# Chunk-selecting attention and a softplus feed-forward on one core: entries of a written-out order moved, four given to another engine, filler matmuls counted anew

## The chip, the cores and the metric

One core of one Trainium2 chip runs the whole program. The metric is the device time of one execution in microseconds (us); of several executions the median is taken. The engines are named as the profile names them: PE (TensorE, matmuls; PEld its weight loads), DVE (VectorE), ACT (ScalarE), POOL (GpSimd), SP (SyncE, which issues DMAs).

## The reference

Attention over 4 batches, 8 heads, 768 positions and a head size of 64, in which each query sees only the 6 best of its causal chunks of 32 keys, then a feed-forward layer on all 3072 tokens:

```python
k_min, k_max = k_chunks.min(axis=3), k_chunks.max(axis=3)
ub = np.sum(np.maximum(q * k_min, q * k_max), axis=-1)
ub = np.where(causal, ub, -1e9)
top_chunks = np.argsort(ub, axis=-1)[..., -6:]
scores = np.where(sel & (pos[:, None] >= pos[None, :]), scale * q @ k.T, -1e9)
attn = softmax(scores) @ v
x = attn.transpose(0, 2, 1, 3).reshape(B * S, H * D)
h = x @ w_in
out = (np.maximum(h, 0) + np.log1p(np.exp(-np.abs(h)))) @ w_out
```

## The kernel before, in words

The queries are cut into 12 blocks of 256 (block n is batch n // 3, rows n % 3). For each block the operations are: loads (`ld k`, `ld q`, `ld v`), transposes of k and q (`kT`, `qT` on PE for blocks 0 to 2, `kD`, `qD` as DMA transposes from block 3 on), the chunks' maxima and negated minima (`kx`, `kn`, line 508 or 500, on DVE), their copy into the block-diagonal tile `bd` (line 520 on DVE, line 294 on POOL), copies of k (`kc`) and q (`qc`), the positive and negative parts of q (`qpn`, lines 562 to 566), the bounds of the chunks (`ub`, lines 585 and 589, PE), their six largest (`mx`, line 612), the mask (`raw`, lines 627 and 630, tile mraw), its transpose (`mT`, lines 643 and 649, PE) and copies into the rows below q (`mc`). Then come the scores (`s`, lines 703 and 704, PE, 256 and 128 or 256 columns), the exponential (`ex`, line 711, ACT), the causal cut (`af`, line 721, POOL), attention times v (`av`, line 733, PE), the normalisation (`nm`, lines 746 and 747, DVE), the transpose (`oT`, line 764) and the copy to x (`xc`, DVE or ACT). The feed-forward follows block by block: `h` (line 902, 8 matmuls of 256 columns), `e` (line 907) and `ln` (line 912) on ACT, `y` (lines 932 and 847), `ye` (copy out of PSUM) and `st` (store).

Block 0 is made in two halves (pairs of heads 0, 1 and 2, 3), so its operations stand twice as often. Its k and q come through SP as fp32 into the tile wx (`ld k0.0` to `ld q0.1`) and are cast (`cast k0.1` and so on) to the tile io. All other loads are issued by POOL at line 364. `oh` (line 305) makes the rows that SP spreads with `ohk` (line 332) below q and k; block 0's scores wait for them.

The order of the work is written out. The string `ORDER` is a list of words: the first letter names the engine (P, A, V, G for POOL, S for SP), then comes the operation and, with #, which of its kind. Each engine executes its words in the order of the list; waits come from the data alone. A word `z` with a number stands for filler on PE: matmuls of the tile zero into a bank that nobody reads, n // 4 of 512 columns (line 1018) and n % 4 of 128 columns (line 1020). One unit is thus 128 columns. All the z words stand in the first 28 us.

```python
    for o in order:
        if isinstance(o, int):
            wide = T.zero.unsqueeze(1).to_broadcast([128, 4, 128])
            for _ in range(o // 4):
                nc.tensor.matmul(T.pools["y"].homes[0], T.zero, wide, start=True, stop=True)
            for _ in range(o % 4):
                nc.tensor.matmul(T.pools["y"].homes[0][:, 0:128], T.zero, T.zero, start=True, stop=True)
            continue
        o.inst = o.fn(o.eng)
```

Of the kernel before, what the change touches and what calls it, by code (L numbers as in the profile page):

```python
# [206 lines left out]
Gld_q2.1 Gld_v1.0 Ps0#4 Aex0#4 Gld_v1.1 Gaf0 z8 Ps0#5 Aex0#5 Vmx1 Vraw1 z1 Ps0 Gaf0 Aex0 Pav0 Pav0 Gaf0 Gw_in0 Vnm0
Gaf0 PqT2 Gw_in1 Gld_q3.0 Vcm0 Ps0#7 z8 PmT1 Vmc1 Akc1 Ps0 PoT0 Aex0 Aex0 Axc0 Pav0 Pav0 z7 Ps1#12 Aex1#12 PkT2 PkT2
Ps1#4 Vmc1 Gaf0#6 Gaf0 Gaf0 Aex1#4 Vnm0 Gaf0 Gld_k3.0 Gw_in2 PqT2 Ps1#5 Aex1#5 z3 PoT0 Ps1#7 z1 Ps1 Gcm Pav0#6 Pav0#7
Gvone Vkx2 Vkn2 Vnm0#3 Vbd2 Vxc0 Aqc2 Aex1#7 Aex1 z14 Ps1 Aex1 z4 Ps1#3 Vqpn2 Vqpn2 z2 Ps1 Pav0 Pav0 Aex1#3 Gaf1#1  # L210
PoT0#3 Ps1#15 Vnm0 Vkc2 Aex1 Gaf1 z2 Ps1#8 Pub2 Axc0#3 Aex1#15 Ps1#11 Aex1#8 Aex1#11 Gw_in3 PoT0 Ps1#13 Pav1 z2 Ps1#9
# [843 lines left out]
```

## Time and profile before

| what | value |
|---|---|
| median of 3 runs | 252.55 us (252.5 to 253.54) |
| the profiled execution | 251.79 us, of which its span is 250.1 us |
| around the span | 1.69 us |
| PE busy | 244.2 us, 98% of the span |
| ACT, DVE, POOL busy | 210.8, 175.9 and 121.2 us |
| granted TensorE clock, mean | 1.000 |

The page of the profile gives the busy time of each engine and, in 40 slices, its share; PEclk is the granted TensorE clock in tenths of full speed. Busy time of PE counts filler like any other matmul. The timeline lists instructions in order of time, merged where equal ones follow each other: start, duration, engine, line, operation, tiles, and in brackets the idle time just before with what ended it.

### The profile page before, as it was taken

How to read it: one execution, taken by the hardware profiler on the slowest of the kernel's cores; microseconds unless marked ns; L12 is line 12 of the kernel's file. 1: busy time of each engine (PE TensorE's matmuls, PEld its weight loads, DVE VectorE, ACT ScalarE, POOL GpSimd, SP SyncE). 2: the span in 40 equal slices, each digit the busy share in tenths (PEclk: the TensorE clock that was granted, in tenths of full speed). 3: DMA queues.
4: the chain of work that ended last, by engine and by line, in shares of the span. 5: the costliest groups of instructions: out<-in, count | busy, mean ns of one | idle time of the engine just before them, and what ended most of it. 6: DMA issues, size and time to landing. Idle time of an engine off the chain costs nothing.

```text
span 250.1 us, 7021 instructions
## 1 busy us (share of the span) xinstructions
PE 244.2 (98%) x2754; PEld 201.0 (80%) x2770; DVE 175.9 (70%) x570; ACT 210.8 (84%) x387; POOL 121.2 (48%) x197
## 2 busy tenths in 40 slices
...
PEclk9999999999999999999999999999999999999999
...
GB/s 171 153 158 172 192 176 152 196 155 204 114 141 169 179 160 145 148 175 175 152 175 160 86 144 105 64 7 42 12 97 43 35 177 3 1 86 3 0 85 168
DMA packets 113953, 29.88 MB, mean 119 GB/s; under 512 B 103776, under 2 KB 110944, under 8 KB 113920
## 3 DMA queue, kind: packets, MB, share of 16 engines
...
q8 instruction: 21, 0.34, 0.5%
...
## 4 chain that ended last, share of the span: by engine, by line
PE 91%; DVE 4%; ACT 2%; issue 1%; ACTq 0%
PE ph L902 34%; PE py L932 11%; PE pt L847 9%; PE py L847 8%; PE ps L703 6%; PE po L733 6%; PE ps L704 4%; PE pt L703 2%; PE ph L932 2%; PE pt L733 2%; PE py L1018 2%; PE pt L704 2%; PE pt L585 2%; ACT qt L293 1%; DVE kx L508 1%
## 5 line engine op out<-in xcount | busy, mean ns | idle before, releaser
L902 PE MATMUL ph<-x,w_in_sb 128*128 128x256 bf16 x768 | 97.5, 272 | 0.0
L721 POOL TENSOR_SCALAR_AFFINE_SELECT pt<-pt 128x256 bf16<-128x256 bf16 x96 | 41.0, 451 | 85.8 <-ACT pt L711 85.4
L711 ACT ACTIVATE pt<-ps 128x512 bf16<-128x512 f32 (+1 forms) x145 | 75.5, 550 | 7.7 <-PE ps L704 6.8
L902 PEld LDWEIGHTS <-w_in_sb 128*128 128x128 bf16 x768 | 72.4, 98 | 9.0
L907 ACT ACTIVATE e<-ph 128x512 f32<-128x512 f32 x96 | 56.9, 607 | 13.8 <-PE ph L902 13.6
L912 ACT ACTIVATE g<-e 128x1024 bf16<-128x1024 f32 x48 | 50.6, 1066 | 0.4
L932 PE MATMUL py<-w_out_sb,g 128*128 128x512 bf16 (+1 forms) x129 | 31.5, 365 | 0.8
L733 PEld LDWEIGHTS <-pt 128*128 128x128 bf16 x672 | 28.1, 97 | 2.3
L711 ACT ACTIVATE pt<-pt 128x512 bf16<-128x512 f32 (+1 forms) x47 | 26.3, 572 | 4.0 <-PE pt L704 3.3
L500 DVE TENSOR_REDUCE kx<-kT 128x32 bf16<-128x1024 bf16 x18 | 21.5, 1210 | 6.7 <-DMA kT<-io 6.6
L932 PEld LDWEIGHTS <-g 128*128 128x128 bf16 x176 | 16.3, 97 | 11.8
L733 PE MATMUL po<-v,pt 128*128 128x65 bf16 x502 | 23.5, 193 | 0.0
L847 PEld LDWEIGHTS <-g 128*128 128x128 bf16 x224 | 21.2, 98 | 2.6
L364 POOL DMA_DIRECT2D v<-in_v_dram x24 | 22.1, 923 | 0.1
L364 POOL DMA_DIRECT2D io<-in_k_dram x22 | 20.1, 919 | 0.0
L364 POOL DMA_DIRECT2D io<-in_q_dram x22 | 20.0, 913 | 0.0
L703 PE MATMUL ps<-qt,kb 128*128 128x256 bf16 x73 | 19.2, 272 | 0.0
L703 PE MATMUL ps<-qa,ka 96*128 96x256 bf16 x72 | 18.9, 273 | 0.1
L847 PEld LDWEIGHTS <-df 128*128 128x128 bf16 x168 | 16.0, 98 | 1.8
L704 PE MATMUL ps<-qt,kb 128*128 128x256 bf16 (+1 forms) x73 | 17.4, 245 | 0.0
L704 PE MATMUL ps<-qa,ka 96*128 96x128 bf16 (+1 forms) x72 | 16.8, 240 | 0.0
L747 DVE TENSOR_TENSOR osw<-po,rew 128x256 bf16<-128x256 f32 x37 | 15.7, 425 | 1.3
...
## 6 DMA issues: line engine op xcount, KB each, us to landing
...
```

The lines of the kernel that those rows point to most:

```text
L364: lambda e, t=t: nc.gpsimd.dma_start(out=into(nm, n, t), in_=rows(nm, n, t)),
L500: nc.vector.tensor_reduce(kx.ap[:, :, j].rearrange("d p (t c) -> d t p c", t=NT), kT.ap.rearrange("d p x -> d (p x)").rearrange("d (t p c ...
L703: nc.tensor.matmul(sp.ap[:, 0:QB], kk[0:nr, p, j * 128:(j + 1) * 128], qq, start=True, stop=True)
L704: nc.tensor.matmul(sp.ap[:, QB:w], kk[0:nr, p, (j + 1) * 128:(j + 2) * 128], qq[:, 1] if last else qq, start=True, stop=True)
L711: lambda e, sp=sp, pt=pt, h=h, j=j, w=w: nc.scalar.activation(pt.ap[:, h, j:j + 2].rearrange("k j c -> k (j c)")[:, 0:w], sp.ap[:, 0:w], A ...
L721: nc.gpsimd.affine_select(out=d, in_=d, compare_op=ALU.is_ge, fill=0.0, base=0, channel_multiplier=-1, pattern=[[0, 2], [1, 128]])
L733: nc.tensor.matmul(o[:, u, h], pt.ap[:, h, j, c0:c0 + 128], T.V[i][:, j, 2 * p + h, :], start=(j == 0), stop=(j == t0 + u))
L847: nc.tensor.matmul(bank.ap[:, c * HD:(c + 1) * HD], a(f), w(f), start=start and f == 0, stop=f == HF - 1, skip_group_check=True)
L902: nc.tensor.matmul(o[:, j], T.w_in[:, dt, ft * 128:(ft + 1) * 128], x.ap[:, dt], start=(dt == 0), stop=(dt == KDM - 1))
L907: lambda e, hb=hb, eb=eb, f2=f2: nc.scalar.activation(eb.ap[:, f2 * 512:(f2 + 1) * 512], hb.ap, ACT.Exp),
L912: lambda e, eb=eb, g=g, f4=f4: nc.scalar.activation(g.ap[:, f4 * 4:(f4 + 1) * 4].rearrange("f j c -> f (j c)"), eb.ap, ACT.Ln, bias=1.0),
L932: nc.tensor.matmul(yb.ap[:, 0:c1 - c0], g.ap[:, f, u * 128:(u + 1) * 128], T.w_out[:, f, c0:c1], start=(f == 0), stop=(f == KFF - 1))
```

## The change

The list `ORDER` alone changes. The whole diff is two versions of that string; its first lines are

```diff
-Vzero Sld_k0.0 Acast_k0.0 Vmr0#1 Vkb0 Vmr0 Gvone Gident z32 PkT0 PkT0 Sld_q0.0 Vr4 Gc4 Vbd0 Vkx0 Vkn0 Sld_k0.1
-Vcast_k0.1 Acast_q0.0 z2 PqT0 PqT0 Aqc0 Vbd0#2 Gld_k1.0 Gld_k1.1 Vqpn0 Aqpn0 Sld_q0.1 Acast_q0.1 z33 PqT0 PqT0
...
+Vzero Sld_k0.0 Acast_k0.0 Vmr0#1 Vkb0 Vmr0 Gvone Gident z32 PkT0 PkT0 Sld_q0.0 Vr4 Gc4 Vbd0 Vkx0 Vkn0 Sld_q0.1
+Sld_k0.1 Acast_q0.0 z2 PqT0 Voh PqT0 Aqc0 Gld_k1.0 Gld_k1.1 Vcast_k0.1 Vqpn0 Acast_q0.1 z23 PqT0 PqT0 Gld_q1.0
...
```

Four operations go to another engine: the first `qpn0` of the negative part from ACT to DVE, the second half's `bd0` from POOL to DVE, the second `xc0` from DVE to ACT, and the second `ye1` from DVE to ACT. On SP `ld q0.1` now stands before `ld k0.1`, `oh` on DVE before `cast k0.1`, and POOL's `ld q2.0` behind both halves of `ld k2`. Between 45 and 80 us some twenty words move by a few places: `av2`, `s2`, `h1`, `s3`, `h2`, `y1`, `kc3`, `qac3`, `kc4`, `bd3`, `bd5`, `ln2`, `e2`, `ld k6`, `ld q6`, `ld q7.0`, `st1`. The z words before are 32 2 33 21 3 12 31 8 1 8 7 3 1 14 4 2 2 2 (186 units), now 32 2 23 16 4 13 7 1 4 1 9 1 18 4 2 5 2 (144 units).

The first place is DVE from the first chunk maxima of block 0 (tile kx_103 from the PE tile ph_87) to those of its second half (ph_88); io is the cast input, ohb the rows of `oh`, qpos and qneg the parts of q. Before:

```order
L508 TENSOR_REDUCE kx_103<-ph_87 128x2x8 x2
L294 CAST io_95<-wx 128x4x2x64
L520 TENSOR_REDUCE bd_76<-kx_103 64x4x8 x2
L566 TENSOR_SCALAR qpos_109<-qt_106 128x512
L305 SCALAR_TENSOR_TENSOR ohb<-ident 32x768
L508 TENSOR_REDUCE kx_103<-ph_88 128x2x8 x2
```

and with the change, up to the chunk maxima of block 1 (kx_104):

```order
L508 TENSOR_REDUCE kx_103<-ph_87 128x2x8 x2
L305 SCALAR_TENSOR_TENSOR ohb<-ident 32x768
L294 CAST io_95<-wx 128x4x2x64
L566 TENSOR_SCALAR qpos_109<-qt_106 128x512
L564 TENSOR_SCALAR qneg_110<-qt_106 128x512
L520 TENSOR_REDUCE bd_76<-kx_103 64x4x8 x2
L508 TENSOR_REDUCE kx_103<-ph_88 128x2x8
L608 TENSOR_REDUCE ub_111<-pt_91 128x4
L612 MAX ub_111<-pt_91 128x8 x4
L508 TENSOR_REDUCE kx_103<-ph_88 128x2x8
...
L520 TENSOR_REDUCE bd_76<-kx_103 64x4x8 x2
L508 TENSOR_REDUCE kx_104<-pt_92 128x4x8 x2
```

The rows of `oh` move ahead of the cast, the first qneg comes from ACT, and the second half's copy into bd from POOL.

The second place is ACT among the exponentials of block 1 (tile pt from the PSUM tiles ps), with the copy x that DVE had before; one piece of the difference:

```order
 L711 ACTIVATE pt_113<-ps_85 128x512
 L711 ACTIVATE pt_113<-ps_86 128x384
+L293 COPY x_121<-pt_91 128x256
 L293 COPY qt_106<-ph_88 128x1024
 L711 ACTIVATE pt_113<-ps_85 128x384
```

The copy of the transposed output to x stands on ACT now, ahead of the copy of block 2's q.

The third place is POOL's queue at the start, where io are the tiles of loaded k and q, v that of v, and qa the rows of q of block 0; one piece of the difference:

```order
 L364 DMA io_97<-in_k_dram 128x8x64 x2
 L364 DMA io_98<-in_q_dram 128x8x64 x2
-L364 DMA io_99<-in_q_dram 128x8x64
 L294 COPY qa_105<-qt_106 64x512
 L364 DMA v_70<-in_v_dram 128x8x64 x2
 L294 COPY qa_105<-qt_106 64x512
-L294 COPY bd_76<-kx_103 64x4x8 x2
```

The first copy of qa comes one DMA issue earlier, and the copy into bd is gone from POOL.

## Rows read from the trace of the kernel before

**Rows 1.** The page, its slices of the granted clock.

```profile
PEclk9999999999999999999999999999999999999999
```

**Rows 2.** Stretches, all engines: length, busy us (x count) PE, PEld, DVE, ACT, POOL.

```profile
10.00:15.00 5.00, 4.94 (x51) 2.86 (x50) 4.94 (x20) 4.84 (x8) 4.94 (x8) 1.00 1.85 174
15.00:20.00 5.00, 4.95 (x76) 3.52 (x75) 4.75 (x27) 4.39 (x10) 4.61 (x9) 1.00 1.99 130
...
140.00:160.00 20.00, 20.00 (x232) 18.05 (x230) 18.84 (x73) 16.88 (x33) 3.82 (x9) 1.00 0.67 114
```

**Rows 3.** The same stretches, line 1018 alone (filler of 512 columns): PE, PEld busy.

```profile
10.00:15.00 5.00, 3.03 (x13) 0.94 (x11) 1.00 1.85 174
15.00:20.00 5.00, 1.57 (x5) 0.40 (x5) 1.00 1.99 130
```

**Rows 4.** Waits of PE's weight loads: total us, times, longest.

```profile
PEld L585 <- DVE qneg L564: 0.5, 1, 0.5
PEld L643 <- DVE mraw L630: 0.4, 1, 0.4
```

**Rows 5.** Timeline of DVE, from the cast of block 0's k to its second mask.

```profile
6.35 0.42 DVE L294 CAST io<-wx 128x512 bf16<-128x512 f32 x1
6.68 0.36 DVE L520 TENSOR_REDUCE bd<-kx 64x32 bf16<-64x32 bf16 x2
7.08 0.30 DVE L566 TENSOR_SCALAR qpos<-qt 128x512 bf16<-128x512 bf16 x1
7.30 0.94 DVE L305 SCALAR_TENSOR_TENSOR ohb<-ident 32x768 bf16<-32x768 bf16 x1
8.59 1.29 DVE L508 TENSOR_REDUCE kx<-ph 128x16 bf16<-128x512 bf16 x2 [0.35 <-PE ph L481]
...
14.15 0.43 DVE L566 TENSOR_SCALAR qpos<-qt 128x1024 bf16<-128x1024 bf16 x1
...
14.59 0.18 DVE L630 TENSOR_TENSOR mraw<-pt,ub 128x8 bf16<-128x8 f32 x1
```

**Rows 6.** Timeline of DVE, block 2's parts of q.

```profile
24.32 0.29 DVE L294 COPY x<-pt 128x256 bf16<-128x256 bf16 x1
24.65 0.57 DVE L566 TENSOR_SCALAR qpos<-qt 128x1024 bf16<-128x1024 bf16 x1
25.14 0.62 DVE L564 TENSOR_SCALAR qneg<-qt 128x1024 bf16<-128x1024 bf16 x1
```

**Rows 7.** Timeline of ACT, a copy to x and block 4's positive part of q.

```profile
24.99 0.37 ACT L293 COPY x<-pt 128x256 bf16<-128x256 bf16 x1
...
63.60 1.06 ACT L562 ACTIVATE qpos<-qt 128x1024 bf16<-128x1024 bf16 x1
```

**Rows 8.** Timeline of POOL, start and the cuts beside block 2's q.

```profile
5.30 2.82 POOL L364 DMA_DIRECT2D io<-in_q_dram  x3
8.10 0.63 POOL L294 COPY qa<-qt 64x512 bf16<-64x512 bf16 x1
...
24.53 0.95 POOL L721 TENSOR_SCALAR_AFFINE_SELECT pt<-pt 128x256 bf16<-128x256 bf16 x2 [0.76 <-ACT pt L711]
```

**Rows 9.** Timeline of PE: filler, block 2's bounds, scores of block 3, block 4's bounds.

```profile
1.06 3.59 PE L1018 MATMUL py<-zero 128*128 128x512 bf16 x8 [1.06 <-DVE zero L303]
...
5.63 1.89 PE L1018 MATMUL py<-zero 128*128 128x512 bf16 x8
...
25.36 0.19 PE L585 MATMUL ph<-bd,qpos 128*128 128x48 bf16 x1
25.82 0.20 PE L585 MATMUL ph<-bd,qneg 128*128 128x48 bf16 x1 [0.27 <-DVE qneg L564]
...
63.53 0.27 PE L703 MATMUL ps<-qa,ka 96*128 96x256 bf16 x1
...
63.70 0.27 PE L703 MATMUL ps<-qa,ka 96*128 96x256 bf16 x1
...
64.74 0.18 PE L585 MATMUL pt<-bd,qpos 128*128 128x32 bf16 x1
```

More of the change, by code (lines that the diff above doesn't have):

```diff
@@ L207 @@
[L207 to L211, printed above, removed]
@@ new lines @@
+Gld_q1.1 Vqpn0 Vbd0#2 PkT1 Akc0 PkT0 Sohk Sohk PkT0 Vkx0 Aqc0 Aqpn0#3 Pub0 Aqpn0 Sohk#3 Vmx0 Vkn0 Vraw0 Gqac0 Vbd0#3
+Gld_v0.0 Akc0 Gld_v0.1 PkT1 Akc0#3 Vkx1 Gqac0 Sohk z16 PmT0 Amc0#1 PqT1 z4 PqT1 Amc0 Aqc1 Vkn1 Ps0#2 Vcm0 Aex0#2 Pub0
+Ps0 Vbd1 Vkc1 Vmx0 Vraw0 z13 PmT0 Vqpn1 Vqac1 Aqpn1 z7 Pub1 Aex0 Akc0 Gld_k2.0 Gld_k2.1 Vmc0 Ps0 Vmc0 Aex0 Gld_q2.0
+Gld_q2.1 Gld_v1.0 z1 Ps0#4 Aex0#4 Gld_v1.1 Gaf0 z4 Ps0#5 Aex0#5 Vmx1 Vraw1 z1 Ps0 Gaf0 Aex0 Pav0 Pav0 Gw_in0 Vnm0 Gaf0
+Gaf0 PqT2 Gw_in1 Gld_q3.0 Ps0#7 PmT1 Vmc1 Akc1 Ps0 PoT0 Aex0 Aex0 Axc0 Pav0 Pav0 z9 Ps1#12 Aex1#12 PkT2 PkT2 Ps1#4
@@ new lines @@
+Vmc1 Gaf0#6 Gaf0 Gaf0 Aex1#4 Vnm0 Gaf0 Gld_k3.0 Gw_in2 PqT2 Ps1#5 Aex1#5 PoT0 Ps1#7 z1 Ps1 Gcm Pav0#6 Pav0#7 Gvone
+Vkx2 Vkn2 Vnm0#3 Vbd2 Axc0 Aqc2 Aex1#7 Aex1 z18 Ps1 Aex1 z4 Ps1#3 Vqpn2 Vqpn2 z2 Ps1 Pav0 Pav0 Aex1#3 Gaf1#1 PoT0#3
+Ps1#15 Vnm0 Vkc2 Aex1 Gaf1 z5 Ps1#8 Pub2 Axc0#3 Aex1#15 Ps1#11 Aex1#8 Aex1#11 Gw_in3 PoT0 Ps1#13 Pav1 z2 Ps1#9 Pav1
+Gld_k3.1 Aex1#13 Gw_out0 Gaf1#6 Gaf1 Ps1#14 Axc0 Vmx2 Gaf1#7 Vraw2 Aex1#9 Aex1#14 Ph0 Ps1#10 Aex1#10 Ps1 Vnm1 Gaf1
+Vqac2 Aex1 Ae0 Gaf1 Gld_q3.1 PmT2 Vmc2 Ph0 Gaf1 Pav1#6 Pav1#7 Vnm1#3 Vkc2 Ps2#6 Ae0 Gld_v2.0 Aex2#6 Ps2#8 Aex2#8 Ph0#3
@@ new lines @@
+Aln0 Ps2#2 Pav1 Pav1 Ps2 Aex2 Ph0 SkD3 Vnm1 Vmc2 Ps2#12 Pav1 Pav1 Aex2#2 PoT1 Vxc1 Ae0 Vnm1 Ps2#5 Vbd0 Ph0 Aex2#12
+Aex2#5 Ae0 Ps2#17 PoT1#2 Ps2#14 Aex2#17 PoT1 Vxc1 Vxc1 Ph0 PoT1 Vxc1 Ps2 Aex2#14 Ae0 Ps2#9 Ae0 Aex2 Ph0 Ps2#11 Aex2#9
+Gaf2 Aex2#11 Ae0 Gw_out1 Ph0 Ae0 Ps2 Ps2 Gaf2#4 Gaf2 Gaf2 Ph1 Gaf2#5 Ph1#2 Gld_v2.1 Vkx3 Aex2 Aex2 Ps2#18 Aln0 Ps2
+Gwh0 Gw_out2 Vkn3 Pav2 Gw_out3 Aex2#18 Py0 Aex2 Ae1 Ps2 Aln0 Aex2 Ps2#22 Ph1 Ae1 Aex2#22 Gld_k4.0 Gld_k4.1 Gld_k5.0
+Gwh2 Ae1 Gld_q4.0 Py0 Ps2 Gaf2 SqD3 Ph1#5 Pav2 Gld_q4.1 Aln1 Ps2#20 Ph1#4 Aex2#20 Vnm2 Gld_k5.1 Pav2 Ae1#4 Vbd3 Aex2
@@ new lines @@
+PoT2 Ae1#5 Axc2 Pav2 Aln0 Ps2 Aex2 Vqpn3 Ph1 Vqpn3 Vkc3 Pub3 Vuba3 Vnm2 Vmx3 Ph1 Ps2 Aex2 Ae1 Aln1 Vraw3 Py0 Pav2 Pav2
+Ps2#21 Vwv0 Vkc3 Ae1 Ps2#23 Aex2#23 Py0 Gaf2#7 Aye0 Ph1 Ps2 Vqac3 Vwv6 SmD3 Gwh4#1 Gwh2 Gaf2 Aex2#21 Ae1 Aln1 Aex2
+SkD4 Sohk Gwd2 Vnm2 Vwv2 Py0 Py0 Py0 Py0 PoT2 PoT2 Aye0 Vxc2 Axc2 Aln1 Pav2 Pav2 SqD4 Py1 Py1 Py1 Sohk Skb0 Gld_v3.0
+Vnm2 PoT2 Gld_q5.0 Amc3 Ps3#2 Aex3#2 Ps3#6 Aex3#6 Vkx4 Gld_q5.1 Vkn4 Vxc2 Vwh6#1 Py1 Aqpn4 Ps3 Ph2 Vqpn4 Vbd4 Pub4
+Vmc3 Gld_v3.1 Vuba4 Aye1 Ps3#4 Vmx4 Vraw4 Vqac4 Ae2 Ph2 Aex3#4 Aex3 Vkc4#1 Ps3 Gld_q7.0 Vkc4 Py1 Gld_k6.0 Gld_k6.1
@@ new lines @@
+Gaf3#2 Ae2 Aex3 Ps3#7 SkD5 Aex3#7 SmD4 Ph2 Ae2 Gaf3#1 Vkx5 Aln2 Ps3 Sst1 Ph2#4 Ps3 SqD5 Aex3 Ae2#4 Ph2#5 Ae2#5 Vkn5
+Aex3 Gaf3 Gaf3#4 Aln2#2 Pav3 Pav3 Vnm3 Gaf3#7 Gaf3#6 Gaf3#5 Gld_q6.0 Py1 Gld_v4.0 Gaf3 Gld_v4.1 Ph2 Vmc4 Pav3#6 Pav3#7
+Py1 Vnm3#3 Ae2 Ps4 Ps4#8 Ps4#4 Aln2 Ps4#9 Pav3#4 Pav3#5 Ph2 Vbd5 SkD6 Aex4#4 Vmc4 Aex4 Aex4#8 Aex4#9 Vnm3#2 Ps4 Aex4
+Vqpn5 Vqpn5 Pav3 Pav3 Vnm3 Ps4#3 Py1 Pub5 Aex4#3 Aye1 Ps4 Ps4#11 Aex4#11 Gaf4#5 Ph2 Ps4#15 Ps4 Py2 Vuba5 Vmx5 Vraw5
+Gld_v5.0 Py2 Aex4 Ps4#12 Gaf4#1 Gaf4 Ae2 Ae2 Aln2 Vkx6 Aex4 Aex4#12 Aex4#15 Pav4 Ps4#7 Aex4#7 Py2 Ps4#14 Aex4#14 SxD3
@@ new lines @@
+Ps4 Ps4 Ps4 Vqac5 Pav4 Gld_q6.1 Vkc5#1 Aex4#10 Aex4#13 Ph3 Gaf4#4 Vkn6 Gld_k7.0 Aex4 Ph3 Ae3 Ae3 Aln3 Pav4#4 Vkc5
+Ph3#6 Pav4#5 Gld_k7.1 SmD5 Vmc5 Vnm4 Ps5#18 Gld_k9.0 Gaf4#6 Gld_v8.0 Gld_v5.1 SqD6 Gaf4#7 Gaf4 Sst0#1 SkD7 Ps5
+Gld_k9.1 Gaf4 Ps5#19 Aex5#18 Aex5#19 Aex5 Py2 Vmc5 Ps5#23 Pav4#6 Ps5 Vnm4#2 Pav4#7 Vnm4#3 Ps5#4 Ps5 Ae3#6 Ph3#4 Aex5
+Aex5#23 Aex5 Aex5#4 Pav4 Ps5#12 Ps5#20 Pav4 Aex5#12 Aex5#20 Ps5#6 Ps5#14 Aex5#6 Aex5#14 Ph3 Ps5#10 Ps5#21 Gld_q7.1
+Gld_v7.0 Gaf5#7 Gaf5#6 Ps5#8 Ps5#22 Vwh0 Gld_k8.0 Vye2 Vqpn6 Vqpn6 Py2 Vkc6#1 Vwd6 Vnm4 Vbd6 Vwv4 Ae3#4 Aex5#21 Aex5#8
@@ new lines @@
+Aex5#10 Ps5#9 Ph3#5 Ps5#11 Ae3 Pub6 Ph3#7 SxD4 Gaf5#2 Aex5#22 Gld_q9.0 Aex5#11 Ae3#5 Pav5#6 Ph3 Gaf5#3 Gaf5#4 Gaf5
+Ae3#7 Aex5#9 Vwh6 Vqac6 Vuba6 Vmx6 Vraw6 Aln3#3 Vkx7 Ae3 Vkc6 SmD6 Vkn7 Vkc7#1 Vbd7 Vkc7 Vmc6 Ps5#17 Ps5#16 Ps5#15
+Ps5#7 Aex5#7 Aex5#17 Py2 Py2 Aex5#16 Pav5#7 Aex5#15 Aln3 Gld_k8.1 Ps5#13 Ps5#5 Gld_v6.0 Gld_v6.1 Ps5 Aex5#13 Gaf5#5
+Ph4#2 Ph4 Aex5#5 Vmc6 Pav5#4 Aln3 Ae4 Aex5 Py2 Ps6#2 Ps6 Aex6 Gaf5 Gld_q11.0 SqD7 Aye2 Ae4#2 Gld_k10.0 Pav5#5 Gaf6
+Gld_q9.1 Gld_k10.1 Ph4 Pav5 Pav5 Py3 Ps6 Vnm5 Aex6 Aex6 Ae4 Ph4#4 Ps6#6 Ps6#7 Vnm5#2 Vqpn7 Vqpn7 Aex6#6 Ae4#4 Vnm5#3
@@ new lines @@
+Aex6#7 Pav5 Pav5 Ps6 Aex6 Vnm5 Pub7 SkD9 SkD8 Gaf6 Vuba7 Pav6 Ph4 Ps6#5 Pav6 Ps6 Vmx7 Vraw7 Sst2#1 Gaf6#7 SxD5 Gaf6#3
+Ae4 Aex6 Aex6 Py3 Ph4 Gaf6#6 Gaf6 Pav6 Py3 Vkx9 Ph4 Pav6#6 SmD7 Vnm6 Sst2 Sst1 Aln4 Ae4 Gaf6#5 Gaf6 Aln4 Py3 Pav6#7
+Vdl4 Ph4 Pav6#4 Pav6#5 Aln4 Gwd0 Gld_k11.0 Gld_k11.1 Gld_v11.0 Gld_v7.1 Gld_q8.0 Aye3 Pav6 Vqac7 Vnm6#3 Vmc7 SqD9 Vkn9
+Vkc9 Vnm6#2 Py3 Py3 Ps7#4 Ae4 Ae4 Aln4 Vdd4 Vbd9 Vmc7 Vqpn9 Ps7 Aex7#4 Ps7#12 Aex7#12 Ph5 Ps7 Aex7 Ps7#5 Ph5#4 Py3
+Aex7#5 Aex7 Ae5#4 Ae5 Ps7#9 Ps7#8 Aex7#8 Aex7#9 Ph5#2 Ps7 Aex7 Gld_q8.1 Ph5 Ae5 Ps7 Vde4 Vnm6 Aex7 Ps7#11 Gld_q11.1
@@ new lines @@
+Gld_v10.0 Gaf7#1 Ps7#15 Aex7#15 Aex7#11 Ae5 Py3 Aye3 Aln5 Vqpn9 Vkx8 Vkc9 Pub9 Ph5 Vuba9 Vmx9 Ph5 Py4 Py4 Ps7#10 Vwh4
+Gld_v9.0 Gld_v9.1 Gaf7#2 Gaf7 Pav7 Ps7 Vraw9 Vkn8 Pav7 Vwd4 Ae5#5 Ae5 Aex7#10 Py4#4 Py4 Ph5#7 Aex7 Aln5#2 Ps7 Aex7 Ps7
+Ps7 Py4#5 Py4#6 Gaf7#7 Gaf7#4 Gaf7 Aln5 Gaf7 Py4 Vnm7 Vdh4 Py4 Vbd8 Vkc8 Gld_v10.1 Vdf4 Vqac9 Ph5 Pav7 Aex7#14 Ayr4
+Aex7 SxD6 Sst0 SmD9 Vyz4 Vyv4 Vmc9#1 Amc9 Ae5 SkD10 Pav7#4 Pav7 Vnm7 Py4#12 Py4#13 Aye4 SqD8 Pav7 Ps9#2 Py4 Vnm7 Py4
+Ps9#5 Ps9#4 Aex9#2 Aex9#4 Ae5 Aln5 Aex9#5 Ps9#6 Py4 Ph6 Py4 Ayd4 Ae6 Aex9#6 Gld_q10.0 Gld_v8.1 Gaf7 Vkc8 Vdl5 Vyw4
@@ new lines @@
+Vqpn8 Vyc4 Vqpn8 Pav7 Pav7 Ph6#2 Ps9#3 Aex9#3 Ps9#7 Ae6#2 Aex9#7 Pub8 Ph6 Gaf9#4 Py5 Ps9 Ph6#4 Ps9 Py5 Vkx10 Vnm7 Aex9
+Ae6 Vde5 Gld_v11.1 Gld_q10.1 Gyx4 Vyf4 Vdd5 Vuba8 Vmx8 Vraw8 Gaf9#2 Aex9 Ph6#5 Gaf9#3 Py5#4 Py5#5 Gaf9 Gaf9 Pav9
+Sst3#1 SxD7 Gaf9#7 Gaf9 SqD10 SmD8 SkD11 Sst4#1 Sst4 Sst3 Ae6#4 Aln6 Ae6#5 Ph6#6 Ae6#6 Ph6#7 Ae6#7 Pav9#4 Pav9#5 Pav9
+Ayr5 Vdh5 Vkn10 Vkc10 Vbd10 Vnm9 Vnm9#2 Ph6 Vdf5 Ae6 Aln6 Aln6#3 Vqac8 Aln6 Gaf9 Py5#6 Py5#7 Py5#8 Ph7 Pav9 Pav9 Ae7
+Ph7#2 Vyz5 Py5 Vmc8 Vqpn10 Vqac10 Vqpn10 Vmc8 Ae7#2 Ps8#12 Py5 Py5 Ps8#14 Aex8#12 Py5#12 Ps8 Vnm9 Aex8 Ph7 Ps8#9 Vyv5
@@ new lines @@
+Vyc5 Ps8#6 Pav9 Py5#13 Pav9 Aex8#14 Ps8#11 Ae7 Aex8#6 Aex8#9 Py5 Py5 Ps8#18 Aex8#11 Ps8#7 Aex8#7 Vdl6 Vde6 Vye5 Vnm9
+Aex8#18 Ps8#17 Aex8#17 Pub10 Ph7 Ayd5 Ae7 Ps8 Ps8#23 Aex8#23 Aex8 Ph7 Ps8 Aex8 Vdh6 Vyw5 Vuba10 Vmx10 Vraw10 Vyx5 Vyf5
+Vdf6 Gaf8 Gaf8#5 Ph7#6 Ps8#5 Aex8#5 Vdd6 Gaf8 Ae7#6 Ps8#22 Py6 Py6 Py6 Ps8#15 Ps8#16 Ph7#7 Py6#4 Aln7 Aex8#16 Aex8#22
+Ps8#10 Py6#5 Ps8#8 Py6#6 SxD9 Ae7 Aex8#10 Gaf8#3 Gaf8#4 Py6 Ps8#4 Ae7#7 Vkx11 Vkn11 SmD10 Ayr6 Vyz6 Vmc10 Ph9#2
+Aex8#15 Aex8#4 Aln7 Py6 Aex8#8 Vkc11 Vyv6 Vmc10 Gaf8#7 Ph7 Gaf8 Ps8#19 Ps8#21 Aex8#21 Ps8#20 Py6 Py6 Aex8#20 Aex8#19
@@ new lines @@
+Py6#12 Ps8#13 Aex8#13 Ps8 SqD11 Aex8 Gaf8 Ae7 Py6#13 Ps10#12 Py6 Pav8#2 Ayd6 Ae9#2 Vye6 Pav8#3 Pav8 Pav8 Py6 Ps10#13
+Aex10#12 Aln7#3 Aex10#13 Vyw6 Aln7 Vkc10 Vyc6 Ph9#5 Pav8#6 Ps10 Ps10#8 Pav8#7 Vbd11 Vnm8 Aex10 Vnm8 Vyx6 Vyf6 Vnm8#3
+Vdl7 Ps10#3 Ph9#4 Aex10#3 Ps10 Py7 Aex10 Ps10#5 Ps10#4 Ae9#4 Vqpn11 Vde7 Vqpn11 Pav8 Pav8 Ps10#7 Aex10#4 Py7 Aex10#5
+Aex10#7 Vnm8 Vdh7 Vdd7 Vdf7 Pub11 Py7#4 Py7#5 Ps10#11 Aex10#8 Ps10#9 Ph9 Ae9#5 Aex10#9 Aex10#11 Vyr7 Ps10 Ae9 Aex10
+Py7 Ph9 Vuba11 Py7 Ps10 Gaf10#2 Ps10#15 Vmx11 Ae9 Aln9 Gaf10#1 Gaf10#4 Gaf10#6 Gaf10#5 Gaf10#3 Gaf10 SxD8 Sst6#1
```

90 lines of the change are left out of this document (17 added, 73 removed).

## The prediction

> **What bounds the kernel now.** I read the page first, for the clock: the granted TensorE clock stands at its upper level (2.4 GHz) in every slice [rows 1]. Then the stretches: from 140 to 160 us PE is busy all 20.00 us with real work [rows 2], so there the end is set by PE, and a change of order wins only what PE loses before. The longest waits of its weight loads are 0.5 and 0.4 us, on DVE in both [rows 4]. There PE looks just as full (4.94 of 5.00 us from 10 to 15 us), but 3.03 us of that is wide filler [rows 2, 3]. The reader is to see that the filler covers waiting: what PE waits for at 14.6 us is the mask of block 0's second half, DVE's chain [rows 4]. The timeline of DVE shows that chain: one wait of 0.35 us before 8.59 us, then no other until the mask is written at 14.59 + 0.18 us [rows 5]. Up to there the kernel is bound by DVE, then by DVE, ACT and PE in turn, and once the filler ends by PE alone.
>
> **The change part by part.**
>
> *The start of DVE.* Before, DVE goes cast, copy into bd, qpos, rows of `oh`, and then waits for the second half's chunk maxima until 8.59 us [rows 5]. Now `oh` comes first, and qneg (ACT's until now) is added. From one start to the next the rows cost: cast 6.68 - 6.35 = 0.33, bd 7.08 - 6.68 = 0.40, qpos 7.30 - 7.08 = 0.22; `oh` 0.94 alone, about 0.86 where its tail is covered as qpos's is [rows 5]. A 512-wide qneg on DVE is not in the trace; the nearest row is qpos of the same size, 0.22, and I take that. DVE starts at 6.35 and needs 0.86 + 0.33 + 0.22 + 0.22 + 0.40 = 2.03 us, so the second half's maxima start at 8.38 instead of 8.59: **0.21 us earlier**. With the bare 0.94 it is 0.13, and no more than the 0.35 of the idle row can be won. From there to the mask, DVE loses block 1's qpos (14.15, behind the mask now) of 0.34 to 0.43 and gains POOL's copy into bd, 0.36 to 0.40 by the DVE row of that copy, and a small memset: nothing in sum. That qpos is then in front of block 1's bounds, which need it anyway. I put 0.2 us to PE here, with ends 0 and 0.35.
>
> *Filler.* 42 units fewer, 37 of them ahead of this mask or just behind. A unit costs 1.89 / 8 / 4 = 0.06 us [rows 9], so about 2.5 us of matmuls go. I cost them at **nothing**: PE waits for DVE with or without them, and what hid under filler becomes visible waiting. The five words from 18 on in the list (18 4 2 5 2) have 7 units more than before, 0.4 us; they stand where PE waits for ACT.
>
> *The copy to x, DVE to ACT.* Between 24.32 and 25.14 us DVE does this copy (0.29 us, 0.33 from start to start) ahead of block 2's parts of q, and PE waits for the second of them: 25.82 - 25.36 = 0.46 us between two matmuls of 48 columns [rows 6, 9], the 0.5 of the waits [rows 4]. Without the copy that wait shrinks by 0.33, and with the 0.2 from the start all of the 0.46 could go. Against that ACT, which feeds the score banks that PE waits for between 20 and 25 us, takes over a copy of 0.37 [rows 7] there. In sum between -0.46 and 0; I take **-0.25**, as ACT was relieved of the first qneg before.
>
> *Block 4's bounds.* One pair of score matmuls of block 3 moves from in front of the feed-forward group to behind block 4's bounds, so the bounds come 63.70 - 63.53 = 0.17 us earlier on PE: 64.57 instead of 64.74 [rows 9]. They wait for ACT's qpos, which ends at 63.60 + 1.06 = 64.66 [rows 7]. So PE stands still for about **+0.13 us** (0 to 0.17) where it had not; behind it the same matmuls follow, and nothing gives it back.
>
> *The rest.* `ld q2.0` behind `ld k2` frees one POOL issue, 2.82 / 3 = 0.94 us [rows 8], for v and k2: hidden, since PE waits for masks and exponentials there, not for loads. SP's order of the four first loads only exchanges which half is cast first. The moves between 45 and 80 us, and the second `ye1` on ACT, lie under a PE that has no wait to give back: nothing, and if their cover is gone the loss is a wait like that of block 4.
>
> **The sum.** -0.2 - 0.25 + 0.13 = -0.32 us, from -0.81 to +0.17. The profiled execution took 251.79 us (its span of 250.1 and 1.69 around it), so 251.5; the median of the runs stands 0.76 above it at 252.55, so **252.2 us** for the median. The three runs reach from 252.5 to 253.54, which I let the range share: 251.4 to 253.0 for this case. A measurement of this kernel tells some 0.5%, 1.26 us, from no change; the forecast is no change.
>
> **A rule that speaks against the start of DVE.** Block 2's qpos and qneg take 0.57 and 0.62 us beside a POOL cut that runs from 24.53 to 25.48; the same qpos at 14.15 takes 0.43 [rows 5, 6, 8]. So fast DVE operations lose up to 0.2 us beside POOL work. With the change POOL's first copy of qa (0.63 us) stands one issue earlier, at 8.10 - 0.94 = 7.16 us [rows 8], right beside DVE's cast, qpos and qneg (7.21 to 7.98 in the sum above); before, it ran beside `oh` and DVE's idle time. The Trainium skill (SBUF — State Buffer, Who interferes with whom) says that DVE's copies, casts and tensor_scalar operations in a two-port mode and GpSimd exclude each other, and the one that starts first holds the shared ports for its whole instruction. By that rule DVE stands up to the whole copy behind POOL, and the sum would be -0.32 + 0.63 = +0.31 us; by the 0.2 of the rows it would be about -0.1.
>
> **The rivals.**
>
> 1. *DVE loses its gain to POOL*: the chain to the mask is 0.2 to 0.63 us longer than I count, 252.4 to 252.9 us. For it: the two rows above. Against it: a block lasts only as long as the rest of the other's instruction, and the DVE chain may wait for PE's transposes anyway. Chance 0.2; still no change by the measurement.
>
> 2. *The clock falls* (slower). PE now stands idle where the filler was: from 67 units ahead of block 1's bounds to 40, with DVE no faster. The filler's only effect is to keep PE busy, and the level of 1.2 GHz is in this trace: the first eight wide fillers take 3.59 us, eight later ones 1.89 [rows 9]. Price: from 15 to 20 us PE has up to 4.95 - 1.57 = 3.4 us of real work [rows 2, 3]; at half the clock that is 6.8 in a stretch of 5, 1.8 us over even when all gaps are filled. So 254.0 us, and from about 4.5 us at the lower level on it counts as slower. Against it: real matmuls go on in every microsecond, and no slice of the page shows a fall in its present gaps [rows 1]; but none of those gaps is as long as those that I expect (18 units fewer right before the second mask, so about 1 us). Chance 0.15.
>
> 3. *The filler was on the path* (faster): were PE late and DVE waiting for it, all 42 units would come back, 252.55 - 2.5 = 250.1 us. Against it: DVE has no wait between 8.59 and the mask [rows 5], and PE waits 0.4 us for the mask behind all its filler [rows 4]. Chance 0.06.
>
> **How the numbers follow.** The forecast has 0.59, rival 1 0.2, rival 2 0.15, rival 3 0.06. Faster by over 0.5% (below 251.3) is rival 3 and the lower tail of the forecast, 0.12. Slower (above 253.8) is most of rival 2 and some of the unlooked-for waits after 45 us, 0.16. The range of 8 in 10 leaves out rival 3 and the upper half of rival 2: 251.3 to 253.7 us.
>
> **What would show it.** In the changed profile: DVE's second half's maxima at about 8.4 us, the second mask written near 14.6 us instead of 14.77, and idle time of PE of about a microsecond in front of its transposes; no wait for qneg near 25.5 us; a new wait of 0.1 us of block 4's bounds for ACT; PEclk at 9 throughout. PE then full as before, and everything there 0.2 to 0.5 us earlier. A clock below 9 in slices 2 to 4, a cast or qneg of DVE beyond 0.6 us near 7.5 us, or filler that DVE waits for would make it wrong.

## The result, and the profile after

| | before | after |
|---|---|---|
| median | 252.98 us (252.47 to 254.6, 11 runs) | 256.3 us (254.24 to 256.98, 11 runs) |
| profiled execution, span | 251.79, 250.1 us | 256.35, 254.6 us |
| PE busy | 244.2 us, 98% | 243.2 us, 96% |

The ratio is 1.0111, with an interval from 1.008 to 1.0142: slower, and outside the forecast of 251.3 to 253.7 us. Ratios here and below leave out executions that took over 1.5% longer than the fastest of their kernel. The profile of before turned out to be one of its best executions: in a later series of 32 the median was 253.52 us (251.81 to 255.34).

The page of after, slices of PE and of the granted clock, which answers [rows 1], and the chain that ended last:

```profile
PE   8779999899999999999989999999999999999995
...
PEclk9999999999999999999999999999999999999999
...
PE 77%; DMA 11%; DVE 6%; ACT 3%; issue 1%; POOL 1%; ACTq 0%; DVEq 0%
```

In this execution the clock did not fall. But a tenth of the chain is now DMA: PE waits for transfers. The stretches that answer [rows 2] (length, busy us and count of PE, PEld, DVE, ACT, POOL, clock, DMA share, GB/s) and the waits that answer [rows 4]:

```profile
10.00:15.00 5.00, 2.72 (x34) 1.72 (x33) 4.82 (x18) 4.40 (x8) 5.00 (x7) 1.00 1.91 161
15.00:20.00 5.00, 4.28 (x68) 3.16 (x69) 4.81 (x27) 3.42 (x8) 4.09 (x8) 1.00 1.97 126
```

```profile
PEld L643 <- DVE mraw L630: 2.7, 2, 1.6
...
PEld L585 <- DVE qneg L564: 1.2, 1, 1.2
```

PE stands idle where filler was, as foreseen: 2.28 of 5 us from 10 to 15 us. The 1.2 us for qneg is not block 2's wait of [rows 4], which is gone, but a new one at 129 us. The start of DVE, which answers [rows 5], and POOL beside it:

```profile
6.40 0.93 DVE L305 SCALAR_TENSOR_TENSOR ohb<-ident 32x768 bf16<-32x768 bf16 x1
7.26 0.41 DVE L294 CAST io<-wx 128x512 bf16<-128x512 f32 x1
7.60 0.27 DVE L566 TENSOR_SCALAR qpos<-qt 128x512 bf16<-128x512 bf16 x1
7.80 0.27 DVE L564 TENSOR_SCALAR qneg<-qt 128x512 bf16<-128x512 bf16 x1
8.00 0.36 DVE L520 TENSOR_REDUCE bd<-kx 64x32 bf16<-64x32 bf16 x2
8.61 0.69 DVE L508 TENSOR_REDUCE kx<-ph 128x16 bf16<-128x512 bf16 x1 [0.25 <-PE ph L481]
...
14.95 0.18 DVE L630 TENSOR_TENSOR mraw<-pt,ub 128x8 bf16<-128x8 f32 x1
```

```profile
7.03 1.52 POOL L294 COPY qa<-qt 64x512 bf16<-64x512 bf16 x1
8.49 1.76 POOL L364 DMA_DIRECT2D v<-in_v_dram  x2
```

DVE is ready at 8.36 us, 0.02 before the forecast, but the second half's maxima start at 8.61, after a wait for PE. PE had stood in its own order for the load of k1, whose transposes (pt) come ahead of those of the second half (ph). So the latter come no earlier than before; PE after, then before:

```profile
7.95 0.40 PE L481 MATMUL pt<-ident,io 128*128 128x128 bf16 x4 [0.54 <-DMA io<-in_k_dram]
8.19 0.39 PE L481 MATMUL ph<-ident,io 128*128 128x128 bf16 x4
```

```profile
8.16 0.39 PE L481 MATMUL ph<-ident,io 128*128 128x128 bf16 x4
```

Against the same matmuls in the profile of before, PE is 1.2 us late at 42 us, and then loses in three places. They are PE's timeline of after at 46 and 49 us, at 89 us, and at 129 us:

```profile
46.23 0.59 PE L932 MATMUL py<-w_out_sb,g 128*128 128x512 bf16 x2 [0.23 <-DMA w_out_sb<-in_moe_w_out_dram]
...
49.27 0.37 PE L733 MATMUL po<-v,pt 128*128 128x65 bf16 x7 [0.77 <-DMA v<-in_v_dram]
...
89.00 0.27 PE L703 MATMUL ps<-qa,ka 96*128 96x256 bf16 x1 [0.58 <-DVE qa L294]
...
129.29 0.17 PE L585 MATMUL pt<-bd,qpos 128*128 128x16 bf16 x1 [0.63 <-DVE osw L747]
129.63 0.18 PE L585 MATMUL pt<-bd,qneg 128*128 128x16 bf16 x1 [0.17 <-DVE qneg L564]
```

From start to start these cost 1.3, 0.74 and 1.1 us; with 0.14 for block 4's bounds and the 1.2 that is 4.5 us, the difference of the spans. Behind 130 us nothing is lost or won. At 129 us DVE had stood 3.56 us for q's DMA transpose:

```profile
127.66 0.43 DVE L566 TENSOR_SCALAR qpos<-qt 128x1024 bf16<-128x1024 bf16 x1 [3.56 <-DMA qt<-io]
```

So two questions: which part of the change makes it, and how can something in the first 50 us make waits at 89 and 129 us.

### The profile page after: what moved, and what is told of

It is laid out like the page before. It is cut to its first block, busy times and chain, and to the rows that moved or that the text cites. A ratio compares the mean times of both kernels' runs of the same rounds, so it can differ in the third digit from the quotient of the medians.

```text
span 254.6 us, 6990 instructions
## 1 busy us (share of the span) xinstructions
PE 243.2 (96%) x2739; PEld 199.9 (78%) x2755; DVE 176.8 (69%) x571; ACT 211.1 (83%) x388; POOL 121.6 (48%) x195
## 4 chain that ended last, share of the span: by engine, by line
PE 77%; DMA 11%; DVE 6%; ACT 3%; issue 1%; POOL 1%; ACTq 0%; DVEq 0%
PE ph L902 26%; PE pt L847 9%; PE py L932 8%; PE py L847 8%; PE ps L703 5%; PE po L733 5%; DMA v<-in_v_dram 4%; DMA qt<-io 4%; PE ps L704 3%; DMA mT<-mraw 2%; PE ph L932 2%; PE pt L585 2%; PE pt L733 2%; DMA io<-in_k_dram 2%; ACT pt L711 2%; PE pt L703 2%
```

## The experiments

**Which half?** The order is cut at the first `SkD3`, near 40 us, where both lists hold the same operations.

```diff
-Vkx0 Vkn0 Sld_k0.1
+Vkx0 Vkn0 Sld_q0.1
...
 Ph0 SkD3 Vnm1
```

> The changed order up to the first DMA transpose of block 3 (about 40 us: zeros, loads of q2, three of the four changes of engine), the old order behind it. Theory A (DVE ends its start 1.0 us late, POOL's cuts and with them its weight loads follow 1.2 us late, and PE then waits for w_out and v at 46 and 49 us): +1.0 and +1.3, so about +2.4 us against before. Rival B (the start costs only what DVE loses, the waits for loads at 46 us come from the moved operations behind 40 us): about +1.0 us. Rival C (neither half costs much alone; a late start only uses up a slack that the second half has taken away): below +0.6 us.

Measured 1.0085 (1.0047 to 1.0123). The other half, old order up to that word and new order behind it:

```diff
 Ph0 SkD3 Vnm1
...
-Ph1#5 Gld_q4.1 Aln1 Ps2#20 Pav2
+Ph1#5 Pav2 Gld_q4.1 Aln1 Ps2#20
```

> The old order up to the first DMA transpose of block 3, the changed one behind it (some twenty words between 45 and 80 us, the second ye1 on ACT, q6, k6 and q7 loaded in another order). Theory A: the waits at 46 and 49 us are gone, those at 67, 89 and 129 us (0.14, 0.74 and 1.1 us in the changed kernel) stay as far as they come from the moved loads: +1.0 to +2.0 us. Rival B: the waits for loads at 46 and 49 us stand here too: about +3 us. Rival C: below +0.6 us.

Measured 1.0012 (0.9985 to 1.0039). The loss comes with the start (its interval and that of the whole change overlap); behind the old start, the moves between 45 and 80 us, the loads and the second `ye1` cost nothing that can be told.

**The copy to x alone.**

```diff
-Vbd2 Vxc0 Aqc2
+Vbd2 Axc0 Aqc2
```

> The kernel before with one change: the second copy to x (xc0) on ACT instead of DVE. The prediction's term: -0.25 us, from -0.46 to 0. Theory that it is hidden by the loads that follow: 0 at the end, though PE's wait for qneg at 25.8 us is gone.

Measured 1.0008 (0.9979 to 1.0037). The trace shows both a gain and its return. PE's wait for qneg of [rows 4] is gone, and PE gains 0.44 us near 26 us (starts of the same matmuls against the profile of before). Then it stands at 32.6 us, where the profile of before has no gap, because a DVE copy that took 0.53 us at 29.45 us there takes 1.13 here. Timeline of PE and of DVE in this run:

```profile
32.58 0.28 PE L703 MATMUL ps<-qa,ka 96*128 96x256 bf16 x1 [0.35 <-ACT e L907]
```

```profile
30.52 1.13 DVE L294 COPY qa<-qt 64x1024 bf16<-64x1024 bf16 x1
31.67 0.85 DVE L294 COPY qa<-pt 32x512 bf16<-32x512 bf16 x2
```

The view names ACT for this wait; the operand qa was not written until 32.52 us. That costs 0.39 of the 0.44. Ten of the 13 profiles with the new start, whose copy to x is on ACT too, have this wait of 0.33 or 0.34 us at 32 to 33 us; none with that copy on DVE has it.

**The filler alone**: the kernel before with the new numbers.

```diff
-z32 z2 z33 z21 z3 z12 z31 z8 z1 z8 z7 z3 z1 z14 z4 z2 z2 z2
+z32 z2 z23 z16 z4 z13 z7 z1 z4 z1 z9 z1 z18 z4 z2 z5 z2
```

> The kernel before with the changed kernel's 144 units of filler in place of 186, nothing else moved. The prediction's term: 0 us, PE waits where filler stood. Rival, filler was on the path: -1 to -2.5 us. Rival, less filler lets PE's granted clock fall behind the gaps: +1 us or more, and slices of the clock below 9.

Measured 1.01 (1.0062 to 1.0139). The part that I had costed at nothing makes, in this series, as much loss as the whole change. In this profile the clock also fell; the stretches of this run:

```profile
10.00:15.00 5.00, 2.28 (x27) 1.36 (x26) 4.07 (x11) 3.46 (x6) 4.94 (x9) 1.00 1.77 165
15.00:20.00 5.00, 4.69 (x56) 2.87 (x54) 3.56 (x26) 3.09 (x6) 1.25 (x3) 0.66 1.83 121
```

A mean of 0.66 from 15 to 20 us is 3.4 us at the level of 1.2 GHz, behind a stretch in which PE was idle 2.72 of 5 us.

**The old filler in the changed kernel**, and in the changed start with the old rest, the same diff with its signs exchanged.

> The changed kernel with the filler of before (186 units instead of 144, in front of the same matmuls as before), all moved operations and changes of engine kept. Theory F (the filler keeps PE at its upper clock through the waits of the start; with less of it PE falls to the lower level for some 3 us near 15 to 19 us, and everything behind is about 1.4 us or more later): the loss goes, ratio to before 0.995 to 1.001 (-1.2 to +0.3 us), no slice of the clock below 9. Rival G (the moved operations cost by themselves, by DVE's and POOL's longer copies): ratio 1.008 to 1.014, as the changed kernel.

> As the run of the changed start alone (changed order up to about 40 us, old order behind), with the filler of before. Theory F: ratio 0.994 to 1.000, since the new start brought block 0's masks 0.9 us earlier than in the two old starts whose cast was slow too. Rival G: 1.006 or more.

Measured 1.0012 (0.9986 to 1.0038) and 1.0031 (1.0002 to 1.0059): rival G is out. With the old filler the moves and the four changes of engine win nothing; of the two ratios one is just clear of 1. Then a part of the filler each:

```diff
-z23 z16 z4 z13 z7 z1 z4
+z23 z16 z4 z12 z31 z1 z8
```

> The changed kernel with only the filler ahead of block 0's second mask and just behind restored (12 units ahead of its first scores, 31 instead of 13 and 7 ahead of the mask's transpose, 8 instead of 4 behind; 171 in all). Theory F: the waits that let the clock fall lie here (12 to 16 us), so most of the loss goes, ratio 0.997 to 1.003. Rival H (the filler ahead of the first mask counts): 1.008 to 1.014.

```diff
-z23 z16 z4
+z33 z21 z4
```

> The changed kernel with only the filler ahead of the first mask restored (33 instead of 23 units, 21 instead of 16; 159 in all). Theory F: the gaps between 12 and 16 us stay, and the loss with them, ratio 1.007 to 1.014. Rival H: 0.997 to 1.003.

Measured 1.0051 (1.003 to 1.0071) and 1.0039 (1.0014 to 1.0064). Both take away half of the loss or more, which neither theory had said; and the mean clock of both profiles is 1.000. The place of the filler is not it, and the clock not alone.

**Again**, for more profiles: the changed kernel twice, then before with the new filler, then the changed kernel with the old filler.

> The changed kernel once more, for a second profile and more times. Theory F, in the form that the runs so far leave: a fall of the clock is only one way to lose; an execution without a fall loses by waits of PE for loads behind 40 us (in the first profile 1.3 us at 46 to 49, 0.74 at 89, 1.1 at 129). If those waits come from the order itself, they stand here again at the same places, the sum at 3 us. If they come from the DMA's timing of one execution, PE is 1.1 to 1.8 us behind the first profile of before at 40 us, and the waits behind differ in place and size, between 0.6 and 3.4 us in sum.

> As the run before it, a third profile of the changed kernel: the same two readings, and the same numbers.

> The kernel before with 144 units of filler once more. Theory F: ratio 1.007 to 1.014 again; PE at 40 us 1.7 us behind the first profile of before where the clock does not fall, 2.5 or more where it falls. Rival (the first measurement was one bad series): 1.003 or less.

> The changed kernel with the filler of before once more. Theory F: ratio 0.998 to 1.004 again, no execution with a mean clock below 0.997, PE 1.4 to 1.7 us behind the first profile of before at 40 us, and waits for loads of about 1 us in sum behind it. Rival (the filler decides nothing behind 40 us): the sum of these waits scatters here up to 3 us too, as in the changed kernel.

Measured 1.0123 (1.0072 to 1.0175), 1.0118 (1.0065 to 1.0171), 1.0047 (1.0016 to 1.0078) and 1.0036 (1.001 to 1.0062). The waits at 46 and 49 us stand in neither of the two new profiles of the changed kernel: they were of that execution. The waits at 89 us (0.74 us in both) and at 129 us (0.9 and 1.2) stand in both, and in neither of the two profiles with the old filler, though nothing behind 30 us differs in the lists. So they do not come from one execution's timing, and need a cause that reaches from the start to 129 us.

**Filler, or instructions?** Filler is also instructions: 15 matmuls with their weight loads went, and the trace has transfers of a kind of its own, "instruction", whose times differ between these kernels. The next four keep the columns and change the count. In x1 (the changed kernel with old filler) and x3 (before) the narrow units are joined:

```diff
-            for _ in range(o % 4):
-                nc.tensor.matmul(T.pools["y"].homes[0][:, 0:128], T.zero, T.zero, start=True, stop=True)
+            if o % 4:
+                nc.tensor.matmul(T.pools["y"].homes[0][:, 0:128 * (o % 4)], T.zero, wide[:, 0:o % 4], start=True, stop=True)
```

In x2 (the changed kernel as it is) and x4 (before) 5 wide matmuls at the very start become 20 narrow ones, `z32` to `z12` and twenty `z1`.

> The changed kernel with the filler of before (186 units), where the 1 to 3 units behind the wide ones are one matmul of 128 to 384 columns: the same columns in 26 PE instructions fewer than with the old filler, so 4 more than the changed kernel has. Theory I (the place of the loads of PE's instructions decides, by the transfers that they meet): the waits near 89 and 129 us return, 0.7 and 1.1 us; ratio to before 1.005 to 1.010, no fall of the clock. Theory F (only the amount of filler counts): ratio 0.998 to 1.004 as with the old filler, no waits there.

> The changed kernel with its 144 units, of which 20 of the first 32 are matmuls of 128 columns instead of 5 of 512: the same columns, 30 PE instructions more, as many as with the old filler. Theory I: no waits near 89 and 129 us; ratio 1.002 to 1.006, what is left being falls of the clock in some executions. Theory F: ratio 1.008 to 1.014, the waits stand as in the changed kernel.

> The kernel before, its filler of 186 units in 26 PE instructions fewer (the same columns). Theory I: a wait of 0.8 to 0.9 us near 88 us as in the two profiles of the old order with less filler; ratio 1.002 to 1.005. Theory F: 1.000, between 0.998 and 1.002.

> The kernel before, its first 32 units as 3 wide matmuls and 20 narrow ones: 30 PE instructions more. Theory I: the loads of PE's instructions come about 2 to 3 us earlier; the waits change in either direction, by up to 1 us in sum. Theory F: 1.000, between 0.998 and 1.002.

Measured 1.0091 (1.006 to 1.0122), 1.0014 (0.9986 to 1.0041), 1.0049 (1.0016 to 1.0083) and 1.0009 (0.9982 to 1.0035). In the changed kernel that decides it: all the old filler in fewer instructions is slow, the new filler in more instructions is not. Nor is it the start's timing: at 40 us the same matmuls stand within 0.2 us of each other in x1, x2 and the first profile of the changed kernel. In the old order x3 and x4 point the same way, but their intervals overlap. In x1 the wait at 89 us is back, in x2 it is gone. PE's timeline of x1, then of x2, same program order:

```profile
87.37 0.40 PE L733 MATMUL pt<-v,pt 128*128 128x65 bf16 x8
88.77 0.27 PE L703 MATMUL ps<-qa,ka 96*128 96x256 bf16 x1 [1.00 <-DVE qa L294]
```

```profile
87.31 0.40 PE L733 MATMUL pt<-v,pt 128*128 128x65 bf16 x8
87.55 0.27 PE L703 MATMUL ps<-qa,ka 96*128 96x256 bf16 x1
```

The copy to qa waits for the mask's DMA transpose. The view of the transfers shows why that is late. Its queue rows are packets, MB and the time that the packets took as a share of 16 engines; its issue rows end with the us from issue to landing. From x1, first the microsecond from 81 us (issues), then that from 84 us (queues):

```profile
mT<-mraw SPq DMA_TRANSPOSE x1, 6.1
...
q0 software_dynamic: 177, 0.02, 1187.2%
q1 hardware_dynamic: 115, 0.03, 14.6%
q8 instruction: 1, 0.02, 9.4%
```

and the same two of x2:

```profile
mT<-mraw SPq DMA_TRANSPOSE x1, 3.8
...
q0 software_dynamic: 875, 0.11, 176.1%
q1 hardware_dynamic: 191, 0.04, 23.2%
```

In x1 a load of instructions begins at 84.1 us, while POOL's loads of the next q and k move. The 177 packets of POOL's queue that start in this microsecond take 11.87 x 16 / 177 = 1.07 us each; in x2 875 packets take 1.761 x 16 / 875 = 0.03 us. There the instructions came at 81.0 us, when no packet of POOL's queue started (from 80.9 to 81.1 us):

```profile
q1 hardware_dynamic: 125, 0.03, 64.1%
q8 instruction: 1, 0.02, 36.1%
```

The stretch from 84 to 86 us of x1 and then of x2 (as above, the last two numbers are DMA share and GB/s) says it in one row each:

```profile
84.00:86.00 2.00, 2.00 (x27) 1.82 (x26) 1.38 (x2) 2.00 (x6) 2.00 (x4) 1.00 6.07 36
```

```profile
84.00:86.00 2.00, 2.00 (x27) 1.83 (x25) 1.86 (x3) 2.00 (x5) 2.00 (x4) 1.00 1.45 105
```

The transfers move 36 instead of 105 GB/s, the mask lands 2.3 us later after the same issue, and PE stands 1.2 us more. The first profile of the changed kernel has the same: a load of instructions at 84.5 us, 78 GB/s from 84 to 86 us, the wait at 89 us.

The twenty profiles bear this out in part. With at most 2761 weight loads on the page (the table below) this load of instructions comes at 83.1 to 84.6 us, and eight of these ten profiles have a wait of 0.5 to 1.0 us near 89 us. With 2764 and more it comes at 79.6 to 81.9 us, and two of ten have such a wait: x4 (0.63) and the new start with old filler (0.32). The mask's transpose takes 4.9 to 6.1 us to land in the ten with a wait, 3.7 to 4.8 in the ten without. x4 also shows that an earlier load is not safe. Its load begins at 81.9 us, and PE then stands twice, the first time for a DMA transpose (that execution took 255.22 us, the median is 253.77):

```profile
84.97 1.91 PE L902 MATMUL ph<-x,w_in_sb 128*128 128x256 bf16 x16 [0.45 <-DMA x<-osw]
...
88.80 0.27 PE L703 MATMUL ps<-qa,ka 96*128 96x256 bf16 x1 [0.63 <-DVE qa L294]
```

Nor do slow packets always cost: beside its load at 79.6 us before has 61 packets of POOL's queue at 0.75 us each (from 80 to 81 us, 2.875 x 16 / 61), and the changed kernel with the first mask's filler has 84 at 0.66 us (from 83.5 to 84.5 us, 3.452 x 16 / 84). No wait near 89 us follows in either.

**How many instructions?** The changed kernel with 18 (x5) and with 48 more (x6), by the same splitting of `z32`.

> The changed kernel, its first 32 units as 5 wide and 12 narrow matmuls: 18 PE instructions more, the same columns. Theory I: PE's instructions near 84 us are loaded about 1.5 us earlier, still among the transfers of the masks and loads, or just ahead of them: ratio 1.001 to 1.010; where the load comes ahead of 82 us no wait at 89 us, where behind, one of 0.5 to 1 us. Rival (any addition at the start helps by its time alone): as with 30 more, 1.001 to 1.004.

> The changed kernel, its first 32 units all as narrow matmuls: 48 PE instructions more, the same columns. Theory I: the load comes near 79 to 80 us, no wait at 89 us for it; ratio 0.998 to 1.004, unless one of the other loads of instructions now meets a transfer that PE waits for. Rival: better than with 30 more, 0.999 or less.

Measured 1.003 (1.0003 to 1.0057) and 1.0025 (0.9994 to 1.0055), and neither profile has the waits at 89 or 129 us. So 18 bring back most of it, and 48 show no more than 30. The profile of x6 has waits for w_out and v of 0.7 and 1.6 us at 46 and 50 us, as the first one of the changed kernel.

All runs by the number of weight loads on their page (one for each matmul):

| PEld x | kernels and ratios to before |
|---|---|
| 2755 | changed 1.0111, 1.0123, 1.0118; new start 1.0085; before with new filler 1.01, 1.0047 |
| 2757 | changed, old filler joined 1.0091; before, joined 1.0049 |
| 2758, 2761 | changed, part of the filler: 1.0039, 1.0051 |
| 2764 | changed, 18 instructions more: 1.003 |
| 2770 | changed, 30 more 1.0014; changed, old filler 1.0012, 1.0036; new start, old filler 1.0031; new rest 1.0012; copy to x 1.0008 |
| 2779, 2785 | changed, 48 more 1.0025; before, 30 more 1.0009 |

The clock goes with the other thing, the amount of filler. A mean below 0.995 stood in 38 of 92 executions with 144 units, in 4 of 22 with 159 or 171, in 1 of 94 of my kernels with 186 and in 6 of 157 of before itself. Its price lies between nothing (in x2 the three such executions took 253.83 to 254.23 us, with a median of all of 253.96) and some 1.2 us (in x6, its longest execution left out, medians of 254.93 us for six such and 253.73 for the five others). Both profiles of before with the new filler have a fall: at 40 us PE stands 0.8 to 1.0 us behind the later profiles of the old start, and the wait at 89 us adds 0.9 to 1.0.

No run beats before beyond its interval.

## Why the prediction was wrong

- **"Filler. ... I cost them at nothing"** is the step that failed. Its reason held at the start: in the changed kernel PE is at 40 us 0.24 us earlier with 144 units (first profile, no fall of the clock) than with 186 (first profile with the old filler). What was missing is that 42 units are also 30 instructions, and that their absence moves every later load of instructions. The term measures 1.0 and 0.5% in two series of the old order (2.5 and 1.2 us), falls of the clock included. With all columns kept and no fall, 26 instructions fewer took 0.9% against before in the changed kernel (x1, 2.3 us) and 0.5% in the old order (x3).
- **The start of DVE, -0.2 us**: DVE's sum was right to 0.02 us, but the row of 8.59 us in [rows 5] shows DVE waiting for PE, so a faster DVE alone could win nothing there. PE's transposes for it came at 8.19 instead of 8.16 us, as PE waited for the load of k1. Behind that the copy into bd stands ahead of block 1's maxima, and the second mask came at 14.95 instead of 14.59 us, where I had put "nothing in sum". All six later profiles with the old start have the cast at 0.77 to 0.91 us, not the 0.42 of [rows 5], and `ohb` at 1.40 instead of 0.94. The profile that I summed against had an unusually good start. Against it the later old starts are 1.6 to 1.7 us behind at 40 us where the clock did not fall, and nine of the 13 new starts 1.1 to 1.5: the start itself has not lost.
- **The copy to x, -0.25 us**: the gain was 0.44 us and went back at 32.6 us, a place that I did not follow DVE to.
- **Block 4's bounds, +0.13 us**: measured 0.14 us, in the place and for the reason given. The rows cited give 64.66 - 64.57 = 0.09; the rest of the 0.13 has no working, and that it came so near is luck.
- **The rest, nothing**: right with the old filler, 1.0012. With the new filler the wait at 129 us stands in the three profiles of the whole change, and in none of the new start alone or the new filler alone.
- **The waits of [rows 4]** were not the longest: PE's weight loads also waited 1.1 us for the tile zero, 0.7 for a cast on ACT and 0.5 for a transfer of `oh`'s rows.
- **Rival 1, DVE loses to POOL**: the copies do meet, but here it was POOL that paid, 1.52 us instead of 0.63, while the cast took 0.41; in two of the profiles with the old filler it was the other way, cast 0.80 and 0.82 and qpos 0.71 us, POOL 0.73 and 0.72. Of the 13 profiles with the new start seven are like the first (cast 0.41, POOL 0.94 to 1.52), six like the second (cast 0.80 to 0.83, POOL 0.64 to 0.84). The Trainium skill (SBUF — State Buffer, Who interferes with whom) says that the one that starts first holds the shared ports. The two profiles agree with that, as POOL's copy starts ahead of the cast; whether the first does is not settled: POOL's copy started ahead of the cast there too (7.03 against 7.26 us), but while DVE was still in `ohb`, which ended at 6.40 + 0.93 = 7.33 us, and the same holds for the two.
- **Rival 2, the clock falls**: it does, in 38 of 92 executions with the new filler, but not in the first profile, and the loss stands in x1 where no execution shows a fall. The right sign, and a part of the loss; not the main cause in the changed kernel.
- **Rival 3, filler on the path**: out; nothing got faster.

What stays open: why the load of instructions at 84 us holds up the other queue for a microsecond, when one at 48.8 us in x1 meets POOL's queue and does not (193 packets, 0.1 us each), why no wait follows a load at 83.1 or 83.2 us in two profiles, and by which of the loads the wait at 129 us comes; x1 has only the one at 89 us. Open too is what the new start alone loses (1.0085), as its one profile, an execution of 254.32 us, has neither of the two waits. That the count decides in the changed kernel is shown by x1 and x2; that this collision is how is argued from its time and place and from the twenty profiles, not shown. Nor is it settled what made the wait for w_out near 46 us, which the first profile of the changed kernel shares with those of x3 and x6 alone.
